# Warm-up matmuls at the opening barrier, earlier transposes and a new grouping of the w1 loads in a squared-ReLU feed-forward kernel

## The chip, the cores and the metric

The kernel runs on one core of one Trainium2 chip. The metric is the device time of one execution in microseconds (us), taken as the median of several runs. A profile of one further execution shows when each engine worked: PE is the matrix engine (PEld its weight loads), DVE the vector engine, ACT the scalar engine, POOL the GpSimd engine, and SP the engine that here only issues DMA transfers.

## The reference

With x of 2048 x 576, w1 of 576 x 4608 and w2 of 4608 x 576, all in bfloat16, it computes a feed-forward block whose activation is the square of a ReLU:

```
h   = einsum("bsd,df->bsf", x, w1) + b1
r   = where(h > 0, h, 0)
h   = r * r
out = einsum("bsf,fd->bsd", h, w2) + b2
```

## The kernel before

**The long part.** The 2048 rows of x are cut into four blocks of 512, and the 4608 columns of w1 into 36 tiles of 128. The contraction over 576 is cut into nine pieces of 64 rows, since 576 is nine times 64. Two w1 tiles form a pair: one lies in the lower 64 partitions of the SBUF tile `w1h` (called h = 0), the other in the upper 64 (h = 1), and their matmuls run side by side in the two halves of the PE array. `a_step(b, j)` (matmuls at L198) does pair j for block b: 9 steps of two matmuls, 18 in all, with the h = 0 and the h = 1 matmul alternating, so that the very first two matmuls of a step already need both halves of the pair. ACT then adds b1 and takes the ReLU (L182), DVE squares (L184). After all of h the second product runs (L302 and L316) and the rows go out.

Pairs are worked on in the order j = 2, 3, ..., 17 for block 0; pairs 0 and 1 of block 0 are done in the opening, by other means. For block 0 the weights are still arriving: `load_w1(eng, h, j0, n, ...)` (L99) brings the tiles of n pairs from j0 on for one half h in one DMA of n x 144 KB. All of these are issued by SP, in the order of a list written out by hand, h = 0 and then h = 1 for each entry:

```
for j0, n in ((2, 1), (3, 1), (4, 1), (5, 1), (6, 2), (8, 2), (10, 2), (12, 2), (14, 4)):
    for h in range(2):
        load_w1(nc.sync, h, j0, n, slice(0, NH))
```

After them SP issues DMA transposes of the second block of x and then the remaining loads.

**The opening.** The first block of x must stand transposed in SBUF before anything can be multiplied. Its four row tiles (`load_x`, L92; 144 KB each) and the four quads of w1 (`load_quad`, L95: 128 rows by 512 columns each) come by eight DMAs, four on SP's queue and four on ACT's, in the order x0, x1, quad 0, quad 1, quad 2, x2, x3, quad 3 over both queues. `issue_at_barrier` moves these eight instructions ahead of the barrier with which the program opens, so that they start at once.

At that barrier every engine reports first, and POOL, which writes a few constants before (one of them the bfloat16 one), releases the others. After it POOL makes the identity matrix `ident` that PE transposes need, and PE runs five warm-up matmuls (NWARM = 5, L150) of 128 x 512 on that constant one, into a PSUM bank `wps` that nobody reads.

Then PE works through a list written out by hand. `transpose_chunks(half, cs, engs)` transposes the 128-column chunks cs of two row tiles (half 0: x0 and x1; half 1: x2 and x3) with two PE matmuls per chunk (L167), and the engine named in engs copies each chunk from PSUM to SBUF (L158 on ACT, L160 on DVE). Chunk NC is the last one, with a second copy of a half (L172). `full_mm(half, c)` (L213) multiplies chunk c of that half by quad c: four matmuls of 128 x 256, accumulated in four PSUM banks. `fill(HALF)` (L153) is one more matmul on ones whose result nobody reads. Four matmuls at L239 add the last 64 rows of the contraction, and the opening ends; `a_step(0, 2)` follows. PSUM has eight banks of one tag: `wps`, the four of `full_mm`, and three that the transposes take in turn, together with that of `wps` when it is free.

The order in which the transposes and products stand in the opening:

```
transpose_chunks(0, (0,), (V,))
transpose_chunks(0, (1,), (A,))
fill(HALF)
full_mm(0, 0)
transpose_chunks(0, (2, NC), (A, V))
full_mm(0, 1)
transpose_chunks(0, (3,), (A,))
full_mm(0, 2)
transpose_chunks(1, (0, 1), (V, A))
full_mm(0, 3)
```

Of the kernel before, what the change touches and what calls it, by code (L numbers as in the profile page):

```python
# [11 lines left out]
BF16 = mybir.dt.bfloat16  # L12
# [5 lines left out]
def kernel(  # L18
# [9 lines left out]
    nc = tc.nc  # L28
    P = 128
# [9 lines left out]
    NC = D // P  # L39
    NH = D // H  # L40
    DM = NC * P
    SB = 512
    NSB = S // SB
    RT = SB // P
    HALF = SB // 2
# [4 lines left out]
    const = ctx.enter_context(tc.tile_pool(name="const", bufs=1))  # L50
# [6 lines left out]
    def bank(name):  # L57
        return psum.tile([P, SB], FP32, name=name, tag="bank")
# [8 lines left out]
    at = [0]  # L67
# [29 lines left out]
    def load_w1(eng, h, j0, n, cs):  # L97
        f0 = pairs[j0][h] * P
        eng.dma_start(out=w1h[h * H:(h + 1) * H, cs, j0 * P:(j0 + n) * P], in_=w1_rows[:, cs, f0:f0 + n * P])  # L99

    def load_rest(eng, h):
        eng.dma_start(out=qr[h * H:(h + 1) * H, :], in_=w1[DM:D, 2 * h * P:2 * (h + 1) * P])

# [11 lines left out]
    for h in range(2):  # L115
        load_rest(nc.sync, h)


    for j0, n in ((2, 1), (3, 1), (4, 1), (5, 1), (6, 2), (8, 2), (10, 2), (12, 2), (14, 4)):
        for h in range(2):  # L120
            load_w1(nc.sync, h, j0, n, slice(0, NH))

# [14 lines left out]

    nc.at_finalize(issue_at_barrier)

    ident = const.tile([P, P], BF16, name="ident")  # L140
    make_identity(nc, ident[:])
    b1_rows = const.tile([P, P], BF16, name="b1_rows")
    nc.gpsimd.memset(b1_rows[:], 0.0)
    nc.gpsimd.dma_start(out=b1_rows[0:NFT, :], in_=b1.rearrange("(ft p) -> ft p", p=P))

    ones = nc.const_aps.tensor(1.0, [P, SB], BF16)
    wps = bank("wps")
    NWARM = 5
    for i in range(NWARM):
        nc.tensor.matmul(wps[:], lhsT=ones[:, 0:P], rhs=ones[:], start=(i == 0), stop=(i == NWARM - 1))  # L150

    def fill(n):
        nc.tensor.matmul(wps[:, 0:n], lhsT=ones[:, 0:P], rhs=ones[:, 0:n], start=True, stop=True)  # L153


    def copy_psum(eng, dst, src):
        if eng is nc.scalar:
            nc.scalar.copy(out=dst, in_=src)  # L158
        else:
            nc.vector.tensor_copy(out=dst, in_=src)  # L160

    def transpose_chunks(half, cs, engs):
        tps = [psum.tile([P, HALF], BF16, name="tp", tag="bank") for c in cs]
        for i in range(2):
            for c, tp in zip(cs, tps):
                d0 = c * P if c < NC else D - P
                nc.tensor.transpose(tp[:, i * P:(i + 1) * P], xs[:, 2 * half + i, d0:d0 + P], ident[:])  # L167
        cols = slice(half * HALF, (half + 1) * HALF)
        for c, tp, eng in zip(cs, tps, engs):
            copy_psum(eng, xT[0][:, c if c < NC else 7, cols], tp[:])  # L170
            if c == NC:
                nc.vector.tensor_copy(out=xT[0][0:H, 8, cols], in_=tp[H:P, :])  # L172
# [37 lines left out]
    def full_mm(half, c):  # L210
        cols = slice(half * HALF, (half + 1) * HALF)
        for q in range(4):
            nc.tensor.matmul(bk0[q][:, cols], lhsT=qn[:, c, q * P:(q + 1) * P], rhs=xT[0][:, c, cols],  # L213
                             start=(half == 0 and c == 0), stop=False, skip_group_check=True)

    V, A = nc.vector, nc.scalar
    transpose_chunks(0, (0,), (V,))
    transpose_chunks(0, (1,), (A,))
    fill(HALF)
    full_mm(0, 0)  # L220
    transpose_chunks(0, (2, NC), (A, V))
    full_mm(0, 1)
    transpose_chunks(0, (3,), (A,))
    full_mm(0, 2)
    transpose_chunks(1, (0, 1), (V, A))
    full_mm(0, 3)
# [9 lines left out]
    for i in range(2):  # L236
        for h in range(2):
            rows = slice(h * H, (h + 1) * H)
            nc.tensor.matmul(bk0[2 * h + i][:], lhsT=qr[rows, i * P:(i + 1) * P], rhs=xT[0][rows, place(h, 8), :],  # L239
                             start=False, stop=True, skip_group_check=True)  # L240
# [57 lines left out]
    for pr in range(NSB // 2):  # L298
        pc = bank("pc")
        for ft in range(NFT):  # L300
            for h in range(2):
                nc.tensor.matmul(pc[h * H:(h + 1) * H, :], lhsT=w2(ft, DM, D), rhs=hT_of(2 * pr + h, ft),  # L302
                                 start=(ft == 0), stop=(ft == NFT - 1))
# [52 lines left out]
```

## Time and profile before

| what | value |
|---|---|
| median of 7 runs | 290.5 us (290.22 to 291.19) |
| time of the profiled execution | 290.58 us |
| its span, first to last instruction | 288.8 us |
| PE busy | 284.9 us, 99% of the span |
| ACT busy, DVE busy | 95.6 us (33%), 79.4 us (27%) |
| matmuls of `a_step` (L198) | 1260 in 135.97 us |
| matmuls of the second product (L302, L316) | 144 in 15.66 us and 612 in 124.53 us |
| DMA, first 26 us | about 200 GB/s or more, mean busy share of the 16 DMA engines 70% to 100% |

The span is what the profile's rows lie in; the 1.8 us between it and the profiled time lie outside of all rows. PE is busy almost throughout, so the end is set by the time at which PE gets through its list: whatever makes PE wait anywhere is added to the end, and what an idle ACT, DVE or POOL does costs nothing. The rows of the opening are short, since everything up to the first matmul at L198 lies in the first 9.74 us.

### The profile page before, as it was taken

Reading aid. Unit: us, or ns where it says so; the run is one execution under the profiler, and the core shown is the slowest. Engines: PE = TensorE matmul, PEld = TensorE weight load, DVE = VectorE, ACT = ScalarE, POOL = GpSimd, SP = SyncE. Lnnn points to the kernel's source line nnn. Section 1 sums busy time; section 2 is a strip of 40 time slices with the busy share of each in tenths; the row PEclk is TensorE's granted clock in tenths of the full one; section 3 lists DMA queues with packets and bytes.
Section 4 is the critical chain, followed back from the end, with each engine's and each line's share of the span. In section 5 each row is a group of like instructions: output and inputs, shape, how many; then the busy total and the mean of one; then the engine's idle time right before and its main releaser. Section 6 shows DMA issues by size and latency. Waiting matters only on the chain.

```text
span 288.8 us, 4832 instructions
## 1 busy us (share of the span) xinstructions
PE 284.9 (99%) x2079; PEld 133.3 (46%) x2079; DVE 79.4 (27%) x195; ACT 95.6 (33%) x153; POOL 1.5 (1%) x8
## 2 busy tenths in 40 slices
PE   8999999999999999999999999999999999999996
PEld 5544444444444444444445444444444444444454
DVE  1644454444445444444420011111100111111111
ACT  3666666666666666666620000000000000000000
POOL 2000000000000000000000000000000000000000
DMA  7999999800300006100000000000000000000000
GB/s 207 216 220 194 184 198 202 309 4 2 120 5 2 1 2 194 54 0 2 0 2 19 20 20 20 20 23 3 17 20 23 20 20 20 23 22 20 20 23 20
DMA packets 34229, 18.01 MB, mean 62 GB/s; under 512 B 19348, under 2 KB 34208, under 8 KB 34208
## 3 DMA queue, kind: packets, MB, share of 16 engines
q1 hardware_dynamic: 33600, 17.14, 26.0%
q10 hardware_dynamic: 576, 0.56, 0.6%
q8 instruction: 16, 0.26, 0.4%
q14 instruction: 5, 0.04, 0.0%
q0 software_dynamic: 32, 0.01, 0.0%
HBM read 11.94 MB, written 2.36 MB: 49 GB/s over the span
## 4 chain that ended last, share of the span: by engine, by line
PE 97%; DMA 2%; SPq 0%; DVE 0%; issue 0%
PE ph L198 47%; PE po L316 43%; PE pc L302 5%; DMA w_sb<-in_x_dram 2%; PE ph L213 1%; SPq L95 0%; PE tp L167 0%; PE ph L239 0%; SPq L92 0%; DVE o_sb L318 0%; PE b1T_ps L232 0%; SPq L340 0%
## 5 line engine op out<-in xcount | busy, mean ns | idle before, releaser
L182 ACT ACTIVATE r<-ph,b1T 128x512 bf16<-128x512 f32 x144 | 91.0, 685 | 48.4 <-PE ph L198 46.5
L198 PE MATMUL ph<-w_sb,w1h 64*128 64x512 bf16 x936 | 101.2, 376 | 0.0
L198 PEld LDWEIGHTS <-w1h 64*128 64x128 bf16 x1260 | 61.3, 94 | 74.7
L316 PE MATMUL po<-w_sb,hT 128*128 128x512 bf16 x432 | 93.4, 379 | 0.0
L316 PEld LDWEIGHTS <-hT 128*128 128x128 bf16 x432 | 42.2, 98 | 51.1 <-issue 0.4
L184 DVE TENSOR_TENSOR hT<-r 128x512 bf16<-128x512 bf16 x108 | 46.0, 426 | 54.7 <-ACT r L182 54.4
L318 DVE TENSOR_TENSOR o_sb<-po,b_bc 128x512 bf16<-128x512 f32 (+2 forms) x17 | 11.2, 661 | 116.7 <-PE po L316 116.7
L198 PE MATMUL ph<-xT,w1h 64*128 64x512 bf16 x324 | 35.1, 376 | 0.0
L316 PE MATMUL po<-w_sb,w1h 128*128 128x512 bf16 (+2 forms) x180 | 31.3, 336 | 0.0
L316 PEld LDWEIGHTS <-w1h 128*128 128x128 bf16 x180 | 16.2, 98 | 15.3
L184 DVE TENSOR_TENSOR w1h<-r 128x512 bf16<-128x512 bf16 x36 | 15.3, 426 | 19.6 <-ACT r L182 19.6
L302 PE MATMUL pc<-hT,w_sb 128*64 128x512 bf16 x108 | 15.7, 379 | 0.0
L302 PEld LDWEIGHTS <-w_sb 128*64 128x64 bf16 x144 | 8.1, 110 | 7.6 <-issue 0.4
L302 PE MATMUL pc<-w1h,w_sb 128*64 128x512 bf16 x36 | 7.9, 379 | 0.0
L304 ACT ACTIVATE oc<-pc,b2T 128x512 bf16<-128x512 f32 x2 | 1.4, 687 | 13.7 <-PE pc L302 13.7
L312 DVE COPY o_sb<-oc 128x64 bf16<-128x64 bf16 x16 | 2.8, 172 | 9.3 <-DMA oc<-oc 9.3
L213 PE MATMUL ph<-w_sb 128*128 128x256 bf16 x32 | 4.7, 283 | 0.0
L213 PEld LDWEIGHTS <-w_sb 128*128 128x128 bf16 x32 | 2.9, 101 | 0.9 <-DMA w_sb<-in_w_dram 0.5
L160 DVE COPY w_sb<-tp 128x256 bf16<-128x256 bf16 x5 | 1.5, 292 | 6.3 <-PE tp L167 6.3
L150 PE MATMUL wps<-const-bfloat16-1.0 128*128 128x512 bf16 x5 | 2.3, 621 | 0.8 <-PEq L340 0.8
L167 PE MATMUL tp<-ident,w_sb 128*128 128x128 bf16 x20 | 2.5, 238 | 0.4 <-DMA w_sb<-in_x_dram 0.4
L158 ACT COPY w_sb<-tp 128x256 bf16<-128x256 bf16 x5 | 1.8, 369 | 2.4 <-PE tp L167 2.4
(28 smaller groups left out, 11.3 us busy)
## 6 DMA issues: line engine op xcount, KB each, us to landing
w_sb<-in_w_dram SPq DMA_DIRECT2D x6, 864.0 KB, 7.0
w1h<-in_w_dram SPq DMA_DIRECT2D x10, 288.0 KB, 7.7
out_dram<-o_sb SPq DMA_DIRECT2D x15, 144.0 KB, 1.7
w1h<-in_w_dram SPq DMA_DIRECT2D x8, 144.0 KB, 3.4
w1h<-in_w_dram SPq DMA_DIRECT2D x2, 576.0 KB, 9.5
w_sb<-in_x_dram SPq DMA_DIRECT2D x2, 144.0 KB, 3.6
w_sb<-in_x_dram ACTq DMA_DIRECT2D x2, 144.0 KB, 3.4
w_sb<-in_w_dram SPq DMA_DIRECT2D x2, 128.0 KB, 3.6
```

Of the source, the lines that this page charges most:

```text
L150: nc.tensor.matmul(wps[:], lhsT=ones[:, 0:P], rhs=ones[:], start=(i == 0), stop=(i == NWARM - 1))
L158: nc.scalar.copy(out=dst, in_=src)
L160: nc.vector.tensor_copy(out=dst, in_=src)
L167: nc.tensor.transpose(tp[:, i * P:(i + 1) * P], xs[:, 2 * half + i, d0:d0 + P], ident[:])
L182: nc.scalar.activation(out=r[:], in_=bk[:], func=ACT.Relu, bias=b1T[:, ft:ft + 1], scale=1.0)
L184: nc.vector.tensor_tensor(out=hT_of(b, ft), in0=r3, in1=r3, op=ALU.mult)
L198: nc.tensor.matmul(bk[h][:], lhsT=w1h[rows, c, j * P:(j + 1) * P], rhs=xT[b][rows, place(h, c), :], start=(i == 0), stop=(i == NH - 1))
L213: nc.tensor.matmul(bk0[q][:, cols], lhsT=qn[:, c, q * P:(q + 1) * P], rhs=xT[0][:, c, cols], start=(half == 0 and c == 0), stop=False, ski ...
L302: nc.tensor.matmul(pc[h * H:(h + 1) * H, :], lhsT=w2(ft, DM, D), rhs=hT_of(2 * pr + h, ft), start=(ft == 0), stop=(ft == NFT - 1))
L312: nc.vector.tensor_copy(out=o_sb[:, DM:D], in_=o_tr[pr][:, jj, h * H:(h + 1) * H])
L316: nc.tensor.matmul(po[:, 0:e - a], lhsT=hT_of(b, ft)[:, jj, :], rhs=w2(ft, a, e), start=(ft == 0), stop=(ft == NFT - 1))
L318: nc.vector.tensor_tensor(out=o_sb[:, a:e], in0=po[:, 0:e - a], in1=b2_bc[:, a:e], op=ALU.add)
```

## The change

There are three edits.

- The five warm-up matmuls read a tile `one` of 128 x 1 that DVE fills, in place of the constant that POOL writes. A function run when the program is finished, `warm_at_barrier`, moves that DVE memset and PE's ten instructions (five weight loads and five matmuls) ahead of the two engines' waits at the opening barrier, but behind their reports to it. PE's first weight load waits for DVE's memset.
- `fill` is gone, with its one call. In its place stand the transposes of chunks 2 and NC of the first half, and the transpose of chunk 3 moves from behind `full_mm(0, 1)` to ahead of it.
- In the list of w1 loads, pairs 6 and 7 become two entries of one pair each, and pairs 10 to 13 become one entry of four. There were 18 DMAs and there are 18; the order of the pairs is the same.

```diff
+    NWARM = 5
...
-    for j0, n in ((2, 1), (3, 1), (4, 1), (5, 1), (6, 2), (8, 2), (10, 2), (12, 2), (14, 4)):
+    for j0, n in ((2, 1), (3, 1), (4, 1), (5, 1), (6, 1), (7, 1), (8, 2), (10, 4), (14, 4)):
...
+    one = const.tile([P, 1], BF16, name="one")
+    nc.vector.memset(one[:], 1.0)
+
+    def warm_at_barrier(nc):
+        entry, body = nc.main_func.blocks[:2]
+        for engine, kinds, n in ((mybir.EngineType.DVE, mybir.InstMemset, 1),
+                                 (mybir.EngineType.PE, (mybir.InstLdweights, mybir.InstMatmult), 2 * NWARM)):
+            mine = [i for i in body.instructions if i.engine == engine and not isinstance(i, mybir.InstNoOp)][:n]
+            assert all(isinstance(i, kinds) for i in mine)
+            at = next(k for k, i in enumerate(entry.instructions)
+                      if i.engine == engine and isinstance(i, mybir.InstEventSemaphore))
+            for k, i in enumerate(mine):
+                body.instructions.remove(i)
+                entry.instructions.insert(at + k, i)
+
+    nc.at_finalize(warm_at_barrier)
...
-    ones = nc.const_aps.tensor(1.0, [P, SB], BF16)
+    ones = one[:].to_broadcast([P, SB])
     wps = bank("wps")
-    NWARM = 5
     for i in range(NWARM):
         nc.tensor.matmul(wps[:], lhsT=ones[:, 0:P], rhs=ones[:], start=(i == 0), stop=(i == NWARM - 1))
-
-    def fill(n):
-        nc.tensor.matmul(wps[:, 0:n], lhsT=ones[:, 0:P], rhs=ones[:, 0:n], start=True, stop=True)
...
     transpose_chunks(0, (0,), (V,))
     transpose_chunks(0, (1,), (A,))
-    fill(HALF)
+    transpose_chunks(0, (2,), (A,))
+    transpose_chunks(0, (NC,), (V,))
     full_mm(0, 0)
-    transpose_chunks(0, (2, NC), (A, V))
+    transpose_chunks(0, (3,), (A,))
     full_mm(0, 1)
-    transpose_chunks(0, (3,), (A,))
     full_mm(0, 2)
     transpose_chunks(1, (0, 1), (V, A))
     full_mm(0, 3)
```

## The prediction

> **What bounds the kernel now.** I read the chain of waits that ended last first, since it says where time added or saved counts. Its columns are start and length in us, and what the time went to.
>
> ```profile
> 1.47 4.84 DMA w_sb<-in_x_dram
> 6.31 0.05 issue
> 6.35 0.28 PE tp L167 x2
> 6.64 0.59 PE ph L213 x4
> ...
> 9.90 135.97 PE ph L198 x1260
> 145.88 15.66 PE pc L302 x144
> 161.54 124.53 PE po L316 x612
> ```
>
> Two things are to be seen. From 6.35 us on PE never stops: 1260 matmuls at 135.97/1260 = 0.108 us are 1.943 us for each `a_step`. Before 6.31 the chain is not PE's at all, but the landing of row tile x3. What PE does earlier has slack.
>
> The second view is the timeline of PE and its weight loads in the opening, which gives that slack in order.
>
> ```profile
> 0.75 0.14 PEld L150 LDWEIGHTS <-const-bfloat16-1.0 128*128 128x128 bf16 x2 [0.75 <-issue]
> ...
> 3.29 0.42 PE L153 MATMUL wps<-const-bfloat16-1.0 128*128 128x256 bf16 x1
> 3.67 0.82 PE L213 MATMUL ph<-w_sb 128*128 128x256 bf16 x4
> 4.55 0.60 PE L213 MATMUL ph<-w_sb 128*128 128x256 bf16 x4
> ...
> 5.25 0.33 PEld L213 LDWEIGHTS <-w_sb 128*128 128x128 bf16 x4 [0.17 <-DMA w_sb<-in_w_dram]
> ...
> 6.35 0.11 PEld L167 LDWEIGHTS <-w_sb 128*128 128x128 bf16 x2 [0.54 <-DMA w_sb<-in_x_dram]
> 6.61 0.33 PEld L213 LDWEIGHTS <-w_sb 128*128 128x128 bf16 x4 [0.15 <-DMA w_sb<-in_w_dram]
> ```
>
> PE's weight loads wait for a DMA three times after the first product: at 5.25 for quad 2, at 6.35 for x3, at 6.61 for quad 3. Everything the change moves on PE lies ahead of 5.25, so three landings stand between it and the end.
>
> The third view is SP's timeline with the DMA issues, asked for one issue at a time; an issue's start plus its "us to landing" is when its last byte is there. The lines are the h = 1 load of pairs 12 and 13; the DMA line's columns are count, size, and us to landing.
>
> ```profile
> 17.68 1.42 SPq L99 DMA_DIRECT2D w1h<-in_w_dram  x1
> w1h<-in_w_dram SPq DMA_DIRECT2D x1, 288.0 KB, 8.2
> ```
>
> It lands at 17.68 + 8.2 = 25.9. The same sum, load by load, gives 12.5 (pair 5, h = 1, issue 8.80 + 3.7), 15.9 and 17.3 (pairs 6-7, both halves), 18.6 and 20.0 (8-9), 21.3 and 22.7 (10-11), 24.3 and 25.9 (12-13), 28.4 and 30.0 (14-17). PE begins pair 2 at 9.74, hence pair j at 9.74 + (j - 2) x 1.943: pair 6 at 17.51, pair 8 at 21.40, pair 10 at 25.28, pair 12 at 29.17, pair 14 at 33.06. The margins are 0.2, 1.4, 2.6, 3.3 and 3.0 us; no step waits. The weight load that opens pair 10 shows no wait:
>
> ```profile
> 25.28 0.10 PEld L198 LDWEIGHTS <-w1h 64*128 64x128 bf16 x2
> ```
>
> **The change, part by part.** *Warm-up at the barrier.* The five matmuls start at 0.78 (weights at 0.75). PE reports to the barrier at about 0.3 us, and a POOL memset of 128x1 takes 0.10 us; DVE's has no row, and I bound it by 0.10 and by DVE's shortest copy, about 0.2. The warm-up then starts near 0.4 and ends 0.3 to 0.4 us earlier. What is queued behind PE's wait for DVE is only PE's own barrier wait, which then comes after the release; POOL releases on reports already sent, so `ident`, ACT's table load and SP's issues stay where they are. The first transposes need x0 and x1, which landed at 2.4 and 2.7 (issues at 0.09 and 0.21, 2.3 and 2.5 to landing): most of the shift dies there. Off the path: 0.
>
> *Transposes for filler.* `fill` took PE 0.21 us (a 256-column matmul at the half speed of that moment: 0.82 us for the four at 3.67, whose last two were already faster, against 0.60 later). Four transposes move up and two more by one product; none is added. The first product still needs quad 0, which its weight load waited for until 3.56, so it starts at 3.67 as before. From there to quad 2 at 5.25 PE has less to do than before, and it was early already. Then come x3 at 6.35 and quad 3 at 6.61, and from 6.61 on the two programs are the same on PE. Off the path: 0. If that cover were gone, with all eight loads early, the two edits together would be worth up to 0.4 + 0.2 = 0.6 us. ACT and DVE copy the chunks earlier, with idle time before them; 0.
>
> *The clock.* The five 512-column warm-ups follow each other every 0.43 us, and such a width later takes 0.216 (two half-array matmuls of 0.108): PE runs at half speed until about 4.1 us, 3.3 us after its first matmul, while the profile's clock column says 1.00 throughout. If the switch follows the first matmul it comes near 3.7, and saves nothing since quad 2 is awaited. If it came late, the 32 matmuls of 0.109 and 12 transposes of 0.055 that stand between 3.67 and 9.30 after the change would cost up to twice their 4.1 us; less the idle 0.17 + 0.54 + 0.15, at most 3.3 us. I take 0, from the row: the same number of warm-ups, unbroken. The Trainium skill, "TensorE: Matmul & The Clock Gate", Part 4, says that transposes do not count as PE activity for the gate, and Part 1 that the activity window of about 3.4 us runs freely; by that, replacing a filler by transposes could push the switch a window later, to about 7.5, for an estimated 0.5 to 0.9 us more at 9.74. No row here separates the two.
>
> *The w1 loads.* There are 18 DMAs before and after; SP's issue took 0.64 us for 144 KB and for the first 288 KB loads alike, so its cost is unchanged, and up to pair 9 and again from pair 14 on the bytes come in the same order. Singles took 0.72 us each at their end (11.8 to 12.5), pairs 1.36 (15.9 to 17.3 to 18.6). Four singles in place of two pairs take 2.9 to 3.0 against 2.7: up to +0.3 for all behind. Pairs 6 and 7 gain: pair 6 is whole some 3 us sooner. Pairs 8-9 land at 20.0 to 20.3, needed at 21.40. Pairs 10 to 13 are where it turns. Before, pair 10 was whole at 22.7. Now h = 0 of all four pairs goes first, and h = 1 comes after it in one DMA that reports when its last byte is there: the bytes that before ended with pairs 12-13 at 25.9. But the first two matmuls of pair 10 need both halves, at 25.28. So a margin of 2.6 us becomes a wait. Its bounds: two DMAs of 576 KB, at the 2.5 us that the first 576 KB one took (25.9 to 28.4), behind 20.0, give 25.0: no wait. The landing of the same bytes plus the singles' loss gives 25.9 + 0.3 = 26.2, and with another 0.3, by which the last two pair loads were slower than 1.36, 26.5: a wait of 1.2. I take 25.9, since there the same bytes were moved behind the same bytes; about 215 GB/s from 10 to 26 us, with pairs as with quadruples, says that packet size matters little. The weight loads of the opening began 0.04 us after their landings. Wait: 25.94 - 25.28 = 0.6 us (0 to 1.2). All of PE behind it moves by that, and an earlier start would only lengthen the wait. Next in line is pair 14: 30.0 against 33.06 + 0.6, safe.
>
> **Sum.** Profiled time 290.58 (span 288.8 and 1.8 around it) + 0 + 0 + 0 + 0.6 = 291.2; the median of the runs lies 0.08 below the profiled one, so 291.1.
>
> **The rivals.** *No wait at pair 10* (not slower). The late landing is that of one straggler: of the 16 completions that the trace has for the load of pairs 12-13, h = 1, the middle one came at 22.9, the last but one at 24.0 and the last at 25.9. Without it, or with quadruples at the 2.5 us of the 25.0 above, pair 10 is there in time. From a landing before 25.24 on this decides, and the time is 290.5, 290.4 at best. Against it: the 24.3 and 25.9 landings, 1.6 us apart, are slower than the pairs before them, not faster.
>
> *The earlier warm-up passes through* (faster). If quad 2, x3 and quad 3 were not awaited, PE would reach pair 2 up to 0.6 us sooner: 289.9. It decides if quad 3 is there before about 5.6 and also pair 10's loads before 24.7. Against it: three waits in the trace, and nothing in the change touches those loads.
>
> *The clock switches a window late* (slower). From a start later by more than the 0.6 that pair 10 waits anyway it decides; between nothing and 3.3 - 0.6 = 2.7 us more, near 292 if it hits.
>
> *The change does less than it says*: the built order of instructions has the warm-up ahead of PE's barrier wait and 18 loads as listed, so this has no chance worth counting.
>
> **How the numbers follow.** A measurement of this kernel can tell about 0.2% from no change, 0.58 us: 289.92 to 291.08. The wait at pair 10 has 0.70, with the larger part of its 0 to 1.2 us above that bound: 0.55 slower, 0.15 within. No wait: 0.17, of it 0.16 within and 0.01 faster. Warm-up passing through: 0.10, faster. Clock late: 0.03, slower. Together faster 0.11, same 0.31, slower 0.58. The likeliest case's own range is 290.7 to 291.8; with the case of no wait the low end is 290.0.
>
> **What would show it.** In the profile after: warm-up weights near 0.4 us; the weight loads at 5.25, 6.35 and 6.61 where they were; pair 2 at 9.74; pair 6 without a wait; and one new wait of PE's weight loads at L198 for a w1 DMA, at pair 10, near 25.3 us, of about 0.6 us. The forecast is wrong if L198 shows no such wait, or if pair 2 begins over 0.3 us from 9.74.

## The result, and the profile after

The changed kernel took 291.56 us (median of 14 runs, 290.61 to 292.02), against 290.38 us for the kernel before beside it (36 runs): a ratio of 1.0038, 95% interval 1.0029 to 1.0047. It is slower by some 1.1 us. The profiled execution took 291.75 us with a span of 290.0 us, 1.17 us more than before.

The chain of waits that ended last, of the kernel after (start, length, what):

```profile
0.62 4.33 DMA w_sb<-in_w_dram
...
16.38 10.03 DMA w1h<-in_w_dram
26.41 0.05 issue
26.45 120.61 PE ph L213 x1115
147.06 15.66 PE pc L317 x144
162.72 124.53 PE po L331 x612
```

Before, PE was on this chain without a break from 6.35 us. Now it joins only at 26.45 us, and what it waited for is one load into `w1h`, under way for 10 us. The last two rows kept their lengths: the time was lost ahead of 26.45 us and nowhere else.

PE's weight loads by what they waited for, after (us in total, times, longest):

```profile
PEld L213 <- DMA w1h<-in_w_dram: 1.5, 1, 1.5
PEld L228 <- DMA w_sb<-in_w_dram: 1.5, 1, 1.5
```

The same weight loads in order of time (in brackets the wait ahead of a load, and for what); L213 and L228 are the former L198 and L213:

```profile
0.38 0.13 PEld L169 LDWEIGHTS <-one 128*128 128x128 bf16 x2 [0.38 <-DVE one L144]
2.57 0.71 PEld L182 LDWEIGHTS <-w_sb 128*128 128x128 bf16 x7 [0.24 <-DMA w_sb<-in_x_dram]
4.76 0.33 PEld L228 LDWEIGHTS <-w_sb 128*128 128x128 bf16 x4 [1.48 <-DMA w_sb<-in_w_dram]
...
9.32 0.74 PEld L213 LDWEIGHTS <-w1h 64*128 64x128 bf16 x8
...
26.45 0.33 PEld L213 LDWEIGHTS <-w1h 64*128 64x128 bf16 x6 [1.50 <-DMA w1h<-in_w_dram]
```

The warm-up starts at 0.38 instead of 0.75 us. The first product then waits 1.48 us for quad 0, which happened to land at 4.72 us here (about 3.5 before), and the opening still comes out 0.2 us early: the first matmul of pair 2 is at 9.53 us, before at 9.74. The one new wait is at 26.45 us, at the two matmuls that open pair 10. By the pace of the steps (below) they were due at 25.07, so PE lost 1.38 us there. 1.38 lost less 0.21 gained is 1.17 us, the whole difference of the two profiled times.

SP's timeline and the DMA issues, after, asked for the h = 1 load of pairs 10 to 13:

```profile
16.38 0.64 SPq L99 DMA_DIRECT2D w1h<-in_w_dram  x1
w1h<-in_w_dram SPq DMA_DIRECT2D x1, 576.0 KB, 10.0
```

16.38 + 10.0 is 26.4, and pair 10 was due at 9.53 + 8 x 1.943 = 25.07. A load reports by 16 completions, and it has landed when the last of them is there. This load's have their middle at 25.6 us; those of the two loads ahead of it (pairs 8-9, h = 1, and pairs 10-13, h = 0) at 19.7 and 22.7. Each quadruple, as a load of four pairs is called here, thus took 2.9 to 3.1 us. The forecast had read 2.5 us for the first 576 KB load of the kernel before, from last completion to last completion; by the middle ones that load took 2.8, since the load ahead of it had one very late completion.

### The profile page after: what moved, and what is told of

Read it like the earlier page. It is cut to its first block, busy times and chain, and to the rows that moved or that the text cites. A ratio compares the mean times of both kernels' runs of the same rounds, so it can differ in the third digit from the quotient of the medians.

```text
span 290.0 us, 4831 instructions
## 1 busy us (share of the span) xinstructions
PE 284.6 (98%) x2078; PEld 133.0 (46%) x2078; DVE 79.4 (27%) x196; ACT 95.5 (33%) x153; POOL 1.5 (1%) x8
## 4 chain that ended last, share of the span: by engine, by line
PE 90%; DMA 5%; SPq 4%; issue 0%; ACTq 0%; DVE 0%
PE po L331 43%; PE ph L213 42%; PE pc L317 5%; SPq L99 4%; DMA w1h<-in_w_dram 3%; DMA w_sb<-in_w_dram 1%; ACTq L92 0%; DVE o_sb L333 0%; ACTq L355 0%
## 5 line engine op out<-in xcount | busy, mean ns | idle before, releaser
L213 PE MATMUL ph<-w_sb,w1h 64*128 64x512 bf16 x936 | 101.6, 376 | 1.0 <-DMA w1h<-in_w_dram 1.0
L213 PEld LDWEIGHTS <-w1h 64*128 64x128 bf16 x1260 | 61.3, 94 | 76.0 <-DMA w1h<-in_w_dram 1.5
L213 PE MATMUL ph<-xT,w1h 64*128 64x512 bf16 x324 | 35.3, 376 | 0.0
L228 PE MATMUL ph<-w_sb 128*128 128x256 bf16 x32 | 4.3, 273 | 1.2 <-DMA w_sb<-in_w_dram 1.2
L228 PEld LDWEIGHTS <-w_sb 128*128 128x128 bf16 x32 | 2.8, 98 | 1.7 <-DMA w_sb<-in_w_dram 1.5
L169 PE MATMUL wps<-one 128*128 128x512 bf16 x5 | 2.3, 628 | 0.4 <-DVE one L144 0.4
```

The source lines that it names most:

```text
L213: nc.tensor.matmul(bk[h][:], lhsT=w1h[rows, c, j * P:(j + 1) * P], rhs=xT[b][rows, place(h, c), :], start=(i == 0), stop=(i == NH - 1))
```

## The experiments

All twelve ran on one chip, with the kernel before at 290.43 to 290.53 us beside them. Two questions were open: is the wait at pair 10 the whole loss, and why did the quadruple come later than the forecast had it? The second soon became the larger one.

**The parts alone.** First the changed kernel with the old list of w1 loads, so that only the two edits of the opening stay:

```diff
-    for j0, n in ((2, 1), (3, 1), (4, 1), (5, 1), (6, 1), (7, 1), (8, 2), (10, 4), (14, 4)):
+    for j0, n in ((2, 1), (3, 1), (4, 1), (5, 1), (6, 2), (8, 2), (10, 2), (12, 2), (14, 4)):
```

> The changed kernel with the old list of w1 loads; warm-up and transposes stay changed. Theory A (the quadruple load of pairs 10 to 13 makes pair 10 wait, and that is the whole loss): no wait at L213 for pair 10; pair 2 begins at about 9.5 as in the changed kernel's profile, 0.2 us earlier than before; time 290.2 to 290.5, ratio to before 0.999 to 1.000. Theory B (the two opening edits make quads 0 and 1 land late, by 1.2 us in the changed kernel's profile, and with them the first w1 load, issued at 4.96 instead of 3.99, so that the whole stream runs late): first w1 issue near 5.0 again, pairs 6-7 land near 18.3 and pair 6 waits about 0.9 us; time 291.2.

Measured: 290.37 us, ratio 0.9995 [0.9984, 1.0006]. Pair 2 starts at 9.75 us, and no step waits for w1. The first w1 load is issued at 4.07 us, so the late issue at 4.96 in the profile after was of that execution (theory B falls). The opening's edits alone are worth nothing that can be measured.

Then the kernel before with the new list and nothing else (the same two lines, the other way round):

> The kernel before with nothing but the new list of w1 loads. Theory A: pair 10 (due at 25.28) waits for the h = 1 quadruple, which lands at 25.9 to 26.5; time 291.0 to 291.6, ratio 1.002 to 1.004. Theory B: the stream starts at 4.0, the quadruple lands near 25.4, wait 0.1 or none; time 290.4 to 290.5.

Measured: 290.57 us, ratio 1.0004 [0.9993, 1.0015]. This I had not expected: the list alone costs nothing either. Pair 2 was late in its profile (10.13 us), so that pair 10 was due at 25.67, and the quadruple landed at 25.82. Quad 0 had landed late there (4.15 us), and PE ran at half speed for longer: its 256-column matmuls stood 0.21 us apart until about 6.1 us, where before they had done so until 4.1. One profile with a late opening proves little, so the changed kernel and this one were run again, unedited:

> The changed kernel itself, on one chip with the next three. The new list alone, in e2, cost 0.04%, the opening edits alone, in e1, nothing, and both together 0.38% in the first comparison. Theory C (the first comparison met slower loads, which is of the day or the chip and not of the opening edits; the price is the landing of the quadruple less the time pair 10 is due): here near e2's, 290.5 to 290.9, and the h = 1 quadruple lands within 0.3 us of where it lands in the new list alone. Theory D (the opening edits make the load stream late): again 291.4 to 291.7, with the quadruple landing 0.6 us or more later than in the new list alone. Theory E (the opening edits bring pair 2 forward by 0.2 to 0.4 us, which the wait at pair 10 takes back): the time is set by the landing alone, so it is the same for both kernels when landings are late, and never faster than the new list alone by more than 0.1 us.

> The kernel before with the new list alone, on the same chip as the changed kernel. Theory C: within 0.2 us of the changed kernel. Theory D: 0.6 us or more below it, at 290.5.

Measured: 292.02 us, 1.0047 [1.0029, 1.0065], for the changed kernel; 290.51 us, 1.0003 [0.9992, 1.0015], for the list alone. In this second profile of the changed kernel (292.92 us) PE's weight loads waited for w1 twice:

```profile
21.78 3.56 PEld L213 LDWEIGHTS <-w1h 64*128 64x128 bf16 x36 [0.79 <-DMA w1h<-in_w_dram]
27.61 0.33 PEld L213 LDWEIGHTS <-w1h 64*128 64x128 bf16 x6 [2.27 <-DMA w1h<-in_w_dram]
```

The first is pair 8, due at 9.45 + 6 x 1.943 = 21.11 us, whose h = 1 load landed at 21.74; the second is pair 10, whose quadruple landed at 27.57. So the single wait of the first profile is one form of the loss and not the only one.

In the second profile of the list alone the opening was early (pair 2 at 9.33, pair 10 due at 24.87 us), and still there was no wait, since the load came sooner. SP's timeline and its DMA issue there:

```profile
15.75 0.64 SPq L99 DMA_DIRECT2D w1h<-in_w_dram  x1
w1h<-in_w_dram SPq DMA_DIRECT2D x1, 576.0 KB, 8.9
```

It landed at 24.64 us, against 26.4 and 27.6 after. So neither half of the change costs anything, and both together cost 0.4%. Something in the opening's edits makes the w1 loads slower, and only with the new list does that matter.

**Is it the wait at pair 10?** In the changed kernel, two pair loads per half in place of the quadruple (20 loads in all):

```diff
-(8, 2), (10, 4), (14, 4)):
+(8, 2), (10, 2), (12, 2), (14, 4)):
```

> The changed kernel with pairs 10 to 13 loaded as two entries of two pairs again, singles for 6 and 7 kept: 20 loads. Theory A: pair 10 whole near 23, no wait; 290.2 to 290.5. Theory B: stream late by 1 us, but pair 10 is due at 25.1, so no wait either, and the time is 290.2 to 290.5 as well; what separates the theories here is only the issue time of the first w1 load (4.0 by A, 5.0 by B).

Measured: 290.47 us, 0.9997 [0.9982, 1.0011]; no wait for w1. The whole loss is gone. Next, only the h = 1 quadruple is split, with h = 0 of all four pairs still ahead of it:

```diff
-(8, 2), (10, 4), (14, 4)):
+(8, 2), (14, 4)):
     for h in range(2):
         load_w1(nc.sync, h, j0, n, slice(0, NH))
+        if (h, j0) == (1, 8):
+            load_w1(nc.sync, 0, 10, 4, slice(0, NH))
+            load_w1(nc.sync, 1, 10, 2, slice(0, NH))
+            load_w1(nc.sync, 1, 12, 2, slice(0, NH))
```

> The changed kernel with the h = 0 quadruple kept and the h = 1 quadruple cut into two loads of two pairs: the same bytes in the same order, one report more, after 288 KB of the h = 1 half. Theory A (the report at the end of the quadruple is what pair 10 waits for): pair 10 is whole 1.4 us earlier, the wait at pair 10 is gone or under 0.2 us; time 290.3 to 290.6, below the changed kernel on the same chip by what that one waits. If instead the order of bytes alone mattered, the time would be that of the changed kernel.

Measured: 290.80 us, 1.0011 [1.0003, 1.0020], 1.2 us under the changed kernel. Pairs 10-11 of h = 1 landed at 25.18 and pairs 12-13 at 26.90 us; pair 10, due at 25.06, still began at 25.22. What costs is the one report at the end of four pairs: the bytes that pair 10 needs are there 1.2 us or more sooner when they report by themselves. Then the quadruple was put two pairs earlier. (Pairs 10 and 11 get other w1 tiles than they should in this kernel, since a load of four takes neighbouring columns of w1 and pairs 8 to 11 are not neighbours there. The bytes and loads are as many.)

```diff
-(8, 2), (10, 4), (14, 4)):
+(8, 4), (12, 2), (14, 4)):
```

> The changed kernel with the quadruple moved from pairs 10-13 to pairs 8-11; pairs 12-13 are two again; 18 loads as in the changed one. Theory A: the wait moves with it: none at pair 10, one at pair 8, due at 21.2, until the h = 1 quadruple lands, about two 2.9 us loads behind pair 7 (16.6 in the changed kernel's profile), 22.3 to 23; wait 1.1 to 1.8 us; time 291.4 to 292.2. Theory B: the grouping matters little; as the changed kernel, 291.5, with a wait wherever the stream is 1 us late.

Measured: 292.13 us, 1.0064 [1.0045, 1.0084]. PE's weight loads in order, this kernel:

```profile
22.89 0.11 PEld L213 LDWEIGHTS <-w1h 64*128 64x128 bf16 x4 [1.82 <-DMA w1h<-in_w_dram]
```

The wait followed the quadruple to pair 8, which was due at 21.2 us and began at 22.9, and the 1.7 us came through to the end, less the 0.2 by which the opening was early (profiled time 292.08, before 290.58). That settles the mechanism of the wait.

**Fewer bytes ahead.** In the changed kernel the two small loads that SP issues ahead of w1 (`load_rest`) were put behind the loads of pairs 2 and 3:

```diff
-    for h in range(2):
-        load_rest(nc.sync, h)
...
         load_w1(nc.sync, h, j0, n, slice(0, NH))
+    if j0 == 3:
+        for h in range(2):
+            load_rest(nc.sync, h)
```

> The changed kernel with the two small loads at L104 issued behind the loads of pairs 2 and 3 in place of ahead of them, so that the first w1 load is issued near 2.7 in place of 4.0 to 5.0 and need not wait for the landing of quad 1. If the quadruple is late because the stream starts late, it lands 0.6 to 1.2 us earlier and the wait at pair 10 shrinks by as much: 290.4 to 290.8. If the loads are bound by bandwidth from 2.7 us on, nothing moves at pair 10, and the quads and row tiles of the opening, now sharing the engines with w1, land later: 291 or more.

Measured: 291.48 us, 1.0041 [1.0025, 1.0056]. The first w1 issue came at 3.08 us, against 4.96 and 4.23 in the two profiles of the changed kernel, and the middle completion of the h = 1 quadruple at 24.87, against 25.61 and 25.06. So an issue 1.1 to 1.9 us earlier bought 0.2 to 0.7 us: the loads already follow each other without a gap. (The last completion, 25.60 against 26.41 and 27.57, differs more between the two profiles of one kernel than by this edit.)

This run also shows how far the opening depends on when PE gets up to speed. In it, and in the run with a `one` of 128 bytes further down, PE begins the first product at 3.8 us and then waits for no load until pair 2. The matmuls of the second and third product, in this run (line L227):

```profile
4.90 1.67 PE L227 MATMUL ph<-w_sb 128*128 128x256 bf16 x8
```

And in the run with 128 bytes (line L229):

```profile
4.80 1.04 PE L229 MATMUL ph<-w_sb 128*128 128x256 bf16 x8
```

The distance of the 256-column matmuls falls from 0.21 to 0.11 us at about 6.2 us here and at about 4.7 there, and pair 2 begins at 9.74 and at 9.01. Half speed for 1.5 us more cost 0.7 us, while the granted clock of the profile reads 1.00 in both.

**Why the loads are slower.** Two theories were left. One is that some instruction of the opening slows the loads down. The other is the place of `w1h` in SBUF: the new tile `one` is two bytes wide and is allocated ahead of `w1h` in the same pool, where it takes 32 bytes of each partition. In the built program `w1h`, which began at byte 18304 of each partition, begins at 18336, and so does all behind it move. To tell the two apart: the kernel before with the new list and one tile more, which nothing reads or writes.

```diff
-    for j0, n in ((2, 1), (3, 1), (4, 1), (5, 1), (6, 2), (8, 2), (10, 2), (12, 2), (14, 4)):
+    for j0, n in ((2, 1), (3, 1), (4, 1), (5, 1), (6, 1), (7, 1), (8, 2), (10, 4), (14, 4)):
...
+    pad = const.tile([P, 1], BF16, name="pad")
```

> The kernel before with the new list alone, as in e2 and e6, and an unused tile of 2 bytes ahead of the identity, which moves w1h to 18336 as in the changed kernel; no opening edit. Theory F: quadruples 2.8 to 3.0 us apart, the h = 1 quadruple lands at 26 or later, pair 10 waits; 291.2 to 292.0. Theory G: as e2 and e6, 290.5.

Measured: 291.88 us, 1.0043 [1.0029, 1.0057]. Without one instruction of the opening's edits, the whole loss is there. Its weight loads' waits for w1, and then its DMA issue of the h = 1 quadruple:

```profile
PEld L199 <- DMA w1h<-in_w_dram: 1.6, 1, 1.6
```

```profile
16.19 0.64 SPq L99 DMA_DIRECT2D w1h<-in_w_dram  x1
w1h<-in_w_dram SPq DMA_DIRECT2D x1, 576.0 KB, 10.5
```

It lands at 26.7 us; without the unused tile it had been 25.8 and 24.6. The h = 1 quadruple comes 2.92 us behind the h = 0 one by their middle completions; without the tile it had been 2.70 and 2.65. The theory of an instruction in the opening falls: the 32 bytes do it. The windows view of 10 us of the loads shows it as a rate (window, its length, busy us and instructions of PE, PEld, DVE, ACT, POOL, then granted clock, DMA share, GB/s). The kernel before:

```profile
16.00:26.00 10.00, 10.00 (x96) 4.55 (x94) 4.26 (x10) 6.62 (x11) 0.00 (x0) 1.00 1.18 218
```

The kernel after:

```profile
16.00:26.00 10.00, 9.45 (x87) 4.08 (x83) 4.27 (x11) 6.62 (x12) 0.00 (x0) 1.00 1.08 209
```

The list alone, second run:

```profile
16.00:26.00 10.00, 10.00 (x96) 4.56 (x94) 4.48 (x11) 6.61 (x12) 0.00 (x0) 1.00 1.10 227
```

The list with the unused tile:

```profile
16.00:26.00 10.00, 9.61 (x89) 4.14 (x85) 4.26 (x10) 6.62 (x11) 0.00 (x0) 1.00 1.15 211
```

227 GB/s without the tile (220 in its first run), 211 with it. PE's busy time, 10.00 against 9.61, has the wait. Which step of the address is the good one was tried with the changed kernel and a wider `one`, first of 64 bytes, so that `w1h` begins at 18368:

```diff
-    one = const.tile([P, 1], BF16, name="one")
-    nc.vector.memset(one[:], 1.0)
+    one_w = const.tile([P, 32], BF16, name="one")
+    one = one_w[:, 0:1]
+    nc.vector.memset(one, 1.0)
...
-    ones = one[:].to_broadcast([P, SB])
+    ones = one.to_broadcast([P, SB])
```

> The changed kernel with the tile of the one made 64 bytes wide in place of 2, of which the first 2 are used. The tile of 2 bytes takes 32 bytes of each partition and so moves w1h from byte 18304, a multiple of 64, to 18336, which is not one; with 64 bytes w1h lies at 18368, a multiple of 64 again. In the profiles so far a pair load took 1.28 to 1.40 us where w1h lay at 18304 (before, e2, e6) or the list was old (e1), and 1.45 to 1.50 where it lay at 18336 (e3, e4, e7, e8); a quadruple 2.65 to 2.72 against 2.8 to 3.0. Theory F (the place of w1h slows the loads): quadruple loads 2.65 to 2.75 us apart, the h = 1 quadruple lands near 25, 1 us or more earlier than in the changed kernel, wait at pair 10 under 0.5 us; time 290.4 to 290.8. Theory G (earlier PE work in the opening slows or delays the loads): as the changed kernel, 291.5 to 292.0, quadruples 2.9 us apart.

Measured: 291.99 us, 1.0047 [1.0034, 1.0060], and 212 GB/s in the same window: a miss. A multiple of 64 bytes does not help. Then the same with 64 elements, 128 bytes, `w1h` at 18432:

> The changed kernel with the tile of the one made 128 bytes wide, which puts w1h at 18432, a multiple of 512. Theory F with 64 bytes as the step that matters: as with 64 bytes, 290.4 to 290.8. If larger steps matter too, quadruples come under 2.65 us apart and the wait is gone: 290.2 to 290.4. The Trainium skill, DMA: Bandwidth & Descriptors, How a descriptor splits into AXI transactions, says that pieces are cut at multiples of 256 bytes; by that this one should be faster than all the others, and 18304, 18336 and 18368 alike. Theory G: 291.5 to 292.0.

Measured: 290.60 us, 1.0004 [0.9990, 1.0018]. Its windows view:

```profile
16.00:26.00 10.00, 9.46 (x89) 4.11 (x87) 4.43 (x11) 6.62 (x11) 0.00 (x0) 1.00 1.04 227
```

The rate is back, with every other edit of the change in place. In this execution pair 2 came as early as 9.01 us, and the weight loads show what became of that:

```profile
25.46 0.11 PEld L214 LDWEIGHTS <-w1h 64*128 64x128 bf16 x4 [1.03 <-DMA w1h<-in_w_dram]
```

Pair 10 was due at 24.55 and its load landed at 25.42 us: the 0.7 us that the opening had gained were taken back at pair 10, and 0.2 more. The middle completion of that load came at 24.49, in time; the late ones decided.

Last, the version that seemed best before the result with 128 bytes was known: `one` of 64 bytes, pairs 6 and 7 singly, pairs 10 to 13 as two pair loads per half.

> The version that should be best by what is known: opening edits, the one in 64 bytes, pairs 6 and 7 as singles, and pairs 10 to 13 as two entries of two. No wait by either theory; pair 2 begins at 9.2 to 9.6 as in e3; 290.1 to 290.4, ratio to before 0.998 to 1.000. By F pair loads are 1.3 to 1.4 us apart, by G 1.45 to 1.5 as in e3.

Measured: 290.48 us, 1.0002 [0.9993, 1.0011]: no wait for w1, and no gain over the kernel before. No run was faster than that kernel by more than the noise. Where `w1h` began and what moved, over all kernels; "apart" is from the middle completion of one load to that of the next of its size (without the last load of the list, which took 3.0 to 4.4 us in every kernel):

| `w1h` begins at byte | kernels | GB/s, 16 to 26 us | pair loads, us apart | quadruples, us apart |
|---|---|---|---|---|
| 18304 = 143 x 128 | before, list alone twice | 218, 220, 227 | 1.28 to 1.38 | 2.65 to 2.70 |
| 18336 | after twice, opening alone, the other lists, small loads later, list and pad | 201 to 211 | 1.37 to 1.59 | 2.85 to 2.92 |
| 18368 | 64 bytes wide, twice | 212, 212 | 1.39 to 1.48 | 2.83 to 2.86 |
| 18432 = 144 x 128 | 128 bytes wide | 227 | 1.34 | 2.62 to 2.64 |

The two multiples of 128 are fast, the two others slow; the window and the quadruples show it without overlap, the pair loads nearly so. The Trainium skill, "DMA: Bandwidth & Descriptors", section "How a descriptor splits into AXI transactions", has transactions cut at multiples of 256 bytes, in words that speak of reading. Taken for the writing of `w1h`, that rule would put 18304 with 18336 and 18368, and only 18432 apart. The runs differ: 18304 gave up to 227 GB/s, as 18432 did. Four addresses do not settle which step counts, nor why.

## Why the prediction was right, and where it was not

The sign, the place and the form of the loss were forecast. The kernel is slower by 1.1 us where 0.6 was said, at 291.56 within 290.0 to 291.8. That the time came out so near is in good part luck: without a shift of `w1h` that the forecast did not see, the new list cost nothing.

**Warm-up and transposes, 0.** Right: 0.9995 [0.9984, 1.0006] for both edits alone. The reason given, that the landings of the opening's loads stand in the way, holds only in part. It named quad 2, x3 and quad 3 as the last waits; after, it was quad 0, and none behind it. Over the profiles here quad 0 landed between 3.2 and 4.7 us and pair 2 began between 9.01 and 10.13, with and without the edits; the landings make one part of that spread, the clock the other. So "pair 2 at 9.74" was one execution's number and not a property of the program. It should have been given a range of half a microsecond either way, and the due time of pair 10 with it.

**The clock, 0.** Right for the profile after, and not as a rule. There the 256-column matmuls follow each other every 0.109 us, the full-speed distance, from 4.76 us on. But the row that the term was read from was one execution's. Over the four profiles without the opening's edits the distance fell to 0.109 at 4.1 to 6.1 us, over nine of the ten with them at 4.1 to 6.2 (after, it fell in a wait, between 3.3 and 4.76), always behind the same five warm-ups. With the old list and the opening's edits it fell at 6.1, which is part of why pair 2 began at 9.75 there. A fall 1.5 us later cost 0.7 us of the opening, as shown above. By the Trainium skill, "TensorE: Matmul & The Clock Gate", Part 4, transposes do not count as activity for the gate of PE's clock; from that the forecast had estimated a fall at 7.5 us and a cost of 0.5 to 0.9. No fall is as late here, and since the list alone, with its filler, had one at 6.1, no run shows that the transposes delay it.

**The w1 loads, the wait at pair 10.** Right in its mechanism: due at about 25, the last load at the end of the same bytes, one wait of PE's weight loads, passed through to the end one for one. Splitting the quadruple removes it, moving the quadruple moves it. In the second profile of the changed kernel pair 8 waited as well: its last load came at 21.74, where 20.0 to 20.3 had been said.

**The size of that term** was wrong: a landing at 25.9 became 26.4, and a due time of 25.28 became 25.07; 0.6 us became 1.38 in that execution, above the 1.2 that was given as its bound. The step that failed is the reading of "about 215 GB/s" in the kernel before: it took the rate of the loads as untouched by the change, and so a landing at 25.9 us, where 26.4 and 27.6 were measured. The landing was bounded by rows of a kernel whose `w1h` lay 32 bytes lower. With that address kept, the landing came at 25.82 and 24.64 us. Against the forecast's due time of 25.28 that is a wait of 0.6 us or none, and the time shows none (1.0004 and 1.0003): in the profile with the later landing the opening was late too. The rival "no wait at pair 10", given 0.17, was thus the right forecast of the time for the list as written, and the loss that made the main forecast come true needs a cause that it did not name. The diff showed it: a new tile ahead of `w1h`.

**Singles for pairs 6 and 7.** No wait at either, as said; nor was there one before. The +0.3 us that four singles might cost was not measured by itself.

**The rival with the straggler.** Of the h = 1 quadruple's completions after, the middle one came at 25.6 and the last at 26.4 us. Both are behind 25.07, so a straggler was 0.8 us of the wait and not all of it. In the second profile they came at 25.06 and 27.57, and pair 10 was due at 24.99 by its opening: there the stragglers were nearly the whole wait. So both count. The middle completion goes with the address (23.56 and 24.04 us for the list alone, 24.49 with 128 bytes, 24.87 to 25.61 in the five runs of the new list at 18336 and 18368). The last one follows 0.6 to 2.5 us behind it at either kind of address, and why is open.

What stays open: whether a start at a multiple of 128 bytes is the rule or only fits four addresses; by what mechanism it acts; and whether `w1h` itself or another tile that moved with it is what counts, though the loads that grew slower are those that write it. Not tried: the placement at 18432 with pair loads in place of the quadruple. It may keep an opening as early as 9.01 us from being taken back at pair 10.

## What to carry to other kernels

Merging loads delays the first consumer to the end of the last byte, so work out the landing against the due time of the first matmul that reads any of it, with a spread for both. A tile added to a pool moves all that is allocated behind it: compare the addresses of the large DMA targets before and after a change, and measure an edit with the addresses held, by a dummy tile, before blaming its instructions. When two halves of a change cost nothing each and something together, look for what the one moves and the other has no margin for.

## What the runs showed of the hardware that was not expected

With all tiles from `w1h` on shifted by 32 bytes per partition, the w1 loads lost 4 to 7% of their rate in the window (227 or 220 to 211 GB/s, list alone against list and pad), and a quadruple took 8 to 10% longer (2.92 us against 2.70 and 2.65). A shift by 128 bytes cost nothing (227 GB/s, 2.62 us).

One load's 16 completions can lie far apart: before, those of pairs 12-13, h = 1, had their middle at 22.9 us and their last at 25.9. A landing read from one execution carries that with it.

The time at which PE's matmuls reach the full-speed distance is not a property of the program either: with five unbroken warm-ups it came 3.3 to 5.8 us behind the first matmul, at 4.1 us before and at 6.2 with the small loads later. With the landings it makes the opening vary: behind the same eight loads the first matmul of pair 2 began at 9.01 us in one execution and at 10.13 in another.
